# Issuing the loads of batch 3 at other places in GpSimd's order

## The chip, the core and the metric

The kernel runs on one core of a Trainium2 chip. Five engines work side by side, each through its own queue in order: TensorE (PE, with its weight loads shown as PEld), VectorE (DVE), ScalarE (ACT), GpSimd (POOL) and SyncE (SP). The metric is device time in microseconds (us); the median over runs is what is compared. One execution is profiled.

## The reference, cut to what matters

```
phi(x) = [exp(x @ w_phi - max|x @ w_phi|), exp(-x @ w_phi - max|...|)]
kv  = phi(k)^T v          z = sum over s of phi(k)         (per batch and head)
att = phi(q) kv / (phi(q) . z + 1e-6)
x   = att, heads side by side: 4608 tokens x 512
h   = x @ w_in            (512 -> 2048)
g   = h if h > 0, else exp(min(h, 0)) - 1
out = g @ w_out           (2048 -> 512)
```

There are 8 batches, 8 heads, 576 tokens in each batch and 64 numbers per head. Inputs and output are float32 in memory; the matmuls are bf16.

## The kernel before, in words

The attention is cut into 16 groups of four heads, two groups to a batch, so batch 3 is groups 6 and 7. For each batch, k, q and v are loaded from memory by one transfer each (`load`, line 213, issued at line 216), with a cast to bf16 on the way, and the issuing engine is GpSimd. The tiles `kn`, `qn` and `vn` come from a pool of two buffers each: the tile of batch 3 takes the buffer of batch 1. For groups from 4 on, k and q are transposed by transfers which SyncE issues (`t_dma`, lines 252 to 269), and the transposed `kT` and `qT` feed the matmuls of `k_mm` (line 294), `m_mm` (lines 353 and 368) and `q_mm` (lines 476 and 488). GpSimd also scales v (`v_scale`, line 331), copies the sums' weights (`v_ones`, line 340), and splits the q maxima of groups 0 to 3 into a high and a low half (`m_split`, lines 421 and 422). `kv_mm` (line 516) and `x_mm` (lines 549 and 565) then give the attention output; SyncE transposes that into `xT` (`x_dma`, lines 656 and 663).

The second part runs in 9 chunks of 512 tokens, mixed with the attention of later groups. For each of 16 column tiles, `h_mm` (line 672) fills a PSUM bank, `h_exp` (683, ScalarE) takes its exponential, `h_min` (688, GpSimd) clamps it at 1, and `h_elu` (692, VectorE) joins it with the bank and so lets go of the bank. `o_mm` (700) multiplies with `w_out`, `o_copy` (710) and `o_store` (716) bring the result out. Chunk 0 is worked in half tiles of 256 columns.

The order of everything is written out by hand in the string `ORDER`. Each letter takes the next item of one list of steps, so `e`, `f` and `g` issue the next load of k, q and v, and `E` the next v scaling, and a digit after a letter names the PSUM bank. The order of the letters is the order in which the program is emitted, and with it the order on each engine; nothing reorders it afterwards. Waits between engines are put in from what the instructions read and write.

```
e=(load, [("k", 0, 0, 1), ("k", 0, 1, 2), ("k", 0, 2, 4)]
   + [("k", *x) for x in all_batches[1:]]),
```

The transfers that GpSimd issues share eight completion semaphores in turn, and so do those that SyncE issues. A transfer waits at issue for the one eight places before it in its own series.

Of the kernel before, what the change touches and what calls it, by code (L numbers as in the profile page):

```python
# [19 lines left out]
DFFUV*M2NW6XBBP5Q*M0S4TTM2NNEU6j1kEEUV*j0k*OP2QS4TTM1NW6Xl0S2l1Y4ZTTj5km*mY7ZOP6Q*W3XS0TTp7A5Cp2  # L20
qrqrM3NS0TTissBp4qrj7kA0p3p2CsBqql6mrsrM4Nsp7p3BBM0Nqqp6p2DqqrrrA4BensssOCp0qY7Z*p3qp1qrsrrssrsE
W6XBl2m*p0p4qM2qrsrP1p5Q*DqES6TNM0NsS2TTTM0NFErsEFY6Zp7qrOsA0BBA2BU4UVp7qp6CP5Q*qBt4S0Tforrssp7q
p5CTrsqp6qW2XW0p7ttXDqS2TA0ngrsErsrsEp5p6p7qrtTCp2qFqrrBsp3qqrp5u*BsqssrsrsDFp4qp7qrsErsS0TTS2TT
t6ttA0zzU4CoEUVA2CBBtuBBW4W0p7t6vzXXzzzzM2NA4DqBenvzftrsM0NM2Np7qrstA0BBBCDM2Ntu*O*P7Q*Ct5S2TTt
M6S0TTEEFNtM6NEFU3S0ogEUVA6CtW3TTBBDEp1p0p2XW6Xuqrqqp5qp3p4p7p6srsA0nerrfqqrsssqrsBBM2NqO*rrp5p4
p2qrCsqssDrqp1qp7P3Q*qsp6p5rrssErsFqA2BBM0NCEqp4rrssqrsFt7S0TtS2M5TTTNvvzzzzS0oTTtA5CEU2US0tVu*B
BDFETTwW2XW4Xvt6A0BBCS2Ttttu*S0M4TTA2CDTFt7ttM0NBBA4BBM2NNCEEEgfDFEEztU0UV*A2CDzzp6qBup5qrrW0xR
t4tBp7qEEressoM0M2p6qrtNNW0xp5qsstu*S2M0p7p6TTrsRNqwp4qqrsS2TTyW0xrrssyp5p7qrqrS2TTnnA0CRp6qvvzo
# [793 lines left out]
```

## Time and profile before

| what | value |
|---|---|
| median of 13 runs | 365.07 us |
| lowest and highest | 362.66 and 369.19 us |
| the profiled execution, its own time | 362.66 us |
| its span, first to last instruction | 360.9 us |
| granted TensorE clock | 0.998 |
| PE busy | 340.7 us, 94% of the span |
| DVE, ACT, POOL busy | 268.9, 250.5 and 212.4 us |
| loads issued by GpSimd, bytes written | 18.35 MB |
| transfers issued by SyncE and ScalarE | 20.56 MB |

The profiled execution is the fastest of those shown; 1.8 us of its time lie outside the span. In the views, L216 is line 216 of the kernel; a row of the timeline has the start, the busy time, the engine, the line, the operation with its tiles, and how often it was repeated without a gap. In brackets stands the idle time ahead of it, with what ended it. SPq and POOLq are rows of issuing.

### The profile page before, as it was taken

How to read it: one execution, taken by the hardware profiler on the slowest of the kernel's cores; microseconds unless marked ns; L12 is line 12 of the kernel's file. 1: busy time of each engine (PE TensorE's matmuls, PEld its weight loads, DVE VectorE, ACT ScalarE, POOL GpSimd, SP SyncE). 2: the span in 40 equal slices, each digit the busy share in tenths (PEclk: the TensorE clock that was granted, in tenths of full speed). 3: DMA queues.
4: the chain of work that ended last, by engine and by line, in shares of the span. 5: the costliest groups of instructions: out<-in, count | busy, mean ns of one | idle time of the engine just before them, and what ended most of it. 6: DMA issues, size and time to landing. Idle time of an engine off the chain costs nothing.

```text
span 360.9 us, 9853 instructions
## 1 busy us (share of the span) xinstructions
PE 340.7 (94%) x3912; PEld 187.0 (52%) x3960; DVE 268.9 (75%) x470; ACT 250.5 (69%) x480; POOL 212.4 (59%) x328
## 2 busy tenths in 40 slices
PE   4788899999999999999999999999999999999994
PEld 3576676554455455545455445544555444444442
DVE  4989986978977998789988999988677914543430
ACT  3998978877898598877967987887855405533401
POOL 8754977358818669386868584767826505432400
PEclk9999999999999999999999999999999999999999
DMA  7999998999667964599578994441214221112123
GB/s 106 200 213 172 200 174 142 171 183 141 151 83 115 206 114 86 100 172 166 109 99 143 127 165 67 84 89 31 52 31 91 65 60 29 29 29 60 26 49 74
DMA packets 68479, 39.72 MB, mean 110 GB/s; under 512 B 48336, under 2 KB 62800, under 8 KB 68432
## 3 DMA queue, kind: packets, MB, share of 16 engines
q0 software_dynamic: 15856, 18.35, 32.7%
q1 hardware_dynamic: 52416, 20.56, 31.6%
q8 instruction: 31, 0.51, 0.6%
q10 hardware_dynamic: 160, 0.16, 0.1%
q14 instruction: 16, 0.13, 0.1%
HBM read 36.77 MB, written 9.44 MB: 128 GB/s over the span
## 4 chain that ended last, share of the span: by engine, by line
PE 80%; DVE 8%; ACT 6%; issue 3%; DMA 1%; POOL 1%; ACTq 0%; POOLq 0%; DVEq 0%
PE banks L700 34%; PE banks L672 28%; PE banks L516 5%; PE banks L549 3%; PE banks L476 2%; ACT EK L305 2%; PE banks L294 2%; DVE gT L692 2%; PE banks L353 2%; DVE mk L312 2%; DVE mq L395 2%; PE banks L565 2%; ACT Eq L500 1%; ACT e_sb L683 1%; DMA kn<-in_k_dram 1%
## 5 line engine op out<-in xcount | busy, mean ns | idle before, releaser
L688 POOL TENSOR_SCALAR e_sb<-e_sb 128x512 f32<-128x512 f32 (+1 forms) x160 | 89.9, 572 | 88.1 <-ACT e_sb L683 83.9
L700 PE MATMUL banks<-w_out_sb,gT 128*128 128x512 bf16 x549 | 131.1, 379 | 3.5 <-issue 2.7
L692 DVE SCALAR_TENSOR_TENSOR gT<-e_sb,banks 128x512 bf16<-128x512 f32 (+1 forms) x160 | 94.8, 625 | 36.0 <-POOL e_sb L688 35.5
L672 PE MATMUL banks<-xT,w_in_sb 128*128 128x512 bf16 (+1 forms) x557 | 119.7, 355 | 1.9 <-DVE mq L395 0.9
L683 ACT ACTIVATE e_sb<-banks 128x512 f32<-128x512 f32 (+1 forms) x160 | 87.0, 565 | 36.7 <-PE banks L672 31.9
L672 PEld LDWEIGHTS <-w_in_sb 128*128 128x128 bf16 x640 | 58.9, 98 | 57.8 <-issue 1.9
L700 PEld LDWEIGHTS <-gT 128*128 128x128 bf16 x576 | 52.8, 98 | 61.1 <-issue 2.4
L305 ACT ACTIVATE EK<-banks 128x768 bf16<-128x768 f32 x96 | 73.5, 814 | 13.4 <-PE banks L294 8.8
L500 ACT ACTIVATE Eq<-banks 128x768 bf16<-128x768 f32 (+2 forms) x96 | 72.8, 819 | 12.8 <-PE banks L476 7.8
L331 POOL TENSOR_TENSOR vs<-vn,em 128x576 bf16<-128x576 bf16 x64 | 73.1, 1154 | 12.6 <-ACT em L322 12.0
L312 DVE TENSOR_REDUCE mk<-banks 128x6 f32<-128x768 f32 x48 | 45.1, 951 | 5.4 <-PE banks L294 2.9
L710 ACT COPY o_sb<-banks 128x512 f32<-128x512 f32 x21 | 12.4, 590 | 34.5 <-PE banks L700 32.1
L381 DVE TENSOR_REDUCE mx<-banks 128x6 f32<-128x768 f32 (+1 forms) x30 | 30.6, 1036 | 3.4 <-PE banks L353 3.2
L615 POOL TENSOR_TENSOR xj<-xs,recj 128x448 bf16<-128x448 f32 (+1 forms) x23 | 20.5, 893 | 13.2 <-DVE recj L610 12.3
L594 DVE TENSOR_TENSOR xs<-banks,e 128x455 f32<-128x455 f32 (+1 forms) x30 | 18.1, 603 | 9.3 <-PE banks L549 8.2
L516 PE MATMUL banks<-vs,EK 64*128 64x65 bf16 x1152 | 21.5, 191 | 0.1
L516 PEld LDWEIGHTS <-EK 64*128 64x128 bf16 x1152 | 20.0, 94 | 2.3 <-DVE mx L381 0.8
L549 PEld LDWEIGHTS <-Eq 128*128 128x128 bf16 x400 | 15.9, 98 | 6.2 <-issue 0.3
L599 DVE TENSOR_TENSOR xs<-banks,xs 128x455 f32<-128x455 f32 (+1 forms) x30 | 18.3, 610 | 1.1
L294 PE MATMUL banks<-w_sb,kT 64*128 64x128 bf16 x288 | 16.6, 227 | 2.4 <-DVE kT L247 1.8
L710 DVE COPY o_sb<-banks 128x512 f32<-128x512 f32 x15 | 10.3, 684 | 11.1 <-PE banks L700 11.1
L549 PE MATMUL banks<-kv_sb,Eq 128*128 128x65 bf16 x400 | 17.1, 194 | 0.1
(67 smaller groups left out, 248.4 us busy)
## 6 DMA issues: line engine op xcount, KB each, us to landing
out_dram<-o_sb SPq DMA_DIRECT2D x71, 128.0 KB, 2.4
kn<-in_k_dram POOLq DMA_DIRECT2D x7, 576.0 KB, 9.1
qn<-in_q_dram POOLq DMA_DIRECT2D x7, 576.0 KB, 7.9
vn<-in_v_dram POOLq DMA_DIRECT2D x7, 576.0 KB, 8.3
w_in_sb<-in_moe_w_in_dram POOLq DMA_DIRECT2D x2, 1024.0 KB, 20.0
w_out_sb<-in_moe_w_out_dram POOLq DMA_DIRECT2D x1, 2048.0 KB, 16.3
qn<-in_q_dram POOLq DMA_DIRECT2D x2, 288.0 KB, 7.4
vn<-in_v_dram POOLq DMA_DIRECT2D x2, 288.0 KB, 8.1
```

Of the source, the lines that this page charges most:

```text
L305: nc.scalar.activation(EK[:, sg, 6 * c:6 * c + 6, :].rearrange("p (i r) f -> p r i f", r=2), st["pk", n, c], ACT.Exp, scale=1.0 - 2.0 * sg,)
L312: nc.vector.tensor_reduce(mk[:, 6 * c:6 * c + 6].rearrange("p (i r) -> p r i", r=2), st["pk", n, c], axis=AX.X, op=ALU.max, apply_absolute ...
L331: nc.gpsimd.tensor_tensor(get(("vs", n), new_vs)[:, sg, r, 0:D], st["v", n // 2][:, 2 * (n % 2) + pr], st["em", n][:, sg, r].unsqueeze(2). ...
L381: nc.vector.tensor_reduce(mq.rearrange("p (v r) -> p r v", r=2)[:, :, v0:v1], st["pm", n, c][:, :, 0:v1 - v0, :], axis=AX.X, op=ALU.max, a ...
L500: nc.scalar.activation(Eq[:, sg, :, :, p0 * D:p1 * D].rearrange("p h r x -> p r h x"), st["pq", n, c][:, :, 0:(p1 - p0) * P].rearrange("p ...
L516: nc.tensor.matmul(kv[:, hi, pr, sg, :], EK[rows, sg, pr * NS + s, :], vs[rows, sg, pr * NS + s, :], start=(s == 0), stop=(s == NS - 1),)
L549: nc.tensor.matmul(pn[:, sg, v - v0, :], Eq[:, sg, hi, par, i0 * D:(i0 + 2) * D], kv_sb[:, hi, pr, sg, :], start=True, stop=True,)
L672: nc.tensor.matmul(ph, w_in_sb[:, ct, jt * P:(jt + 1) * P], xT_of(ch)[:, ct, h0:h1], start=(ct == 0), stop=(ct == N_CT - 1),)
L683: nc.scalar.activation(e_sb, st["ph", ch, jt, h0], ACT.Exp)
L688: nc.gpsimd.tensor_scalar(e_sb, e_sb, 1.0, 0.0, op0=ALU.min, op1=ALU.max)
L692: nc.vector.scalar_tensor_tensor(gT[:, jt, h0:h1], st["e", ch, jt, h0], -1.0, st["ph", ch, jt, h0], op0=ALU.add, op1=ALU.max,)
L700: nc.tensor.matmul(po, st["gT", ch][:, jt, tt * P:(tt + 1) * P], w_out_sb[:, jt, :], start=(jt == 0), stop=(jt == N_JT - 1),)
```

## The change

Three letters move in `ORDER`; the rest of the kernel is the same. The load of k of batch 3 moves to just after the second v scaling of group 3. The load of q moves to a place behind two clamps of chunk 0 that follow it. The load of v moves ahead to a place behind the clamp of column tile 14, where the other two had been a few steps earlier. The splits of q maxima of groups 2 and 3 are issued by GpSimd in both kernels. The order of instructions on PE, DVE, ACT and SP is the same in both.

```diff
-p5CTrsqp6qW2XW0p7ttXDqS2TA0ngrsErsrsEp5p6p7qrtTCp2qFqrrBsp3qqrp5u*BsqssrsrsDFp4qp7qrsErsS0TTS2TT
-t6ttA0zzU4CoEUVA2CBBtuBBW4W0p7t6vzXXzzzzM2NA4DqBenvzftrsM0NM2Np7qrstA0BBBCDM2Ntu*O*P7Q*Ct5S2TTt
-M6S0TTEEFNtM6NEFU3S0ogEUVA6CtW3TTBBDEp1p0p2XW6Xuqrqqp5qp3p4p7p6srsA0nerrfqqrsssqrsBBM2NqO*rrp5p4
+p5CTrsqp6qW2XW0p7ttXDqS2TA0ngrsErsrsEep5p6p7qrtTCp2qFqrrfBsp3qqrp5u*BsqssrsrsDFp4qp7qrsErsS0TTS2
+TTt6ttA0zzU4CoEUVA2CBBtuBBW4W0p7t6vzXXzzzzM2NA4DqBnvztrgsM0NM2Np7qrstA0BBBCDM2Ntu*O*P7Q*Ct5S2TTt
+M6S0TTEEFNtM6NEFU3S0oEUVA6CtW3TTBBDEp1p0p2XW6Xuqrqqp5qp3p4p7p6srsA0nerrfqqrsssqrsBBM2NqO*rrp5p4
```

On GpSimd's queue this reads as follows (lines without a sign are context):

```diff
 L331 TensorTensor vs<-vn,em 128x9x64
+L216 DMACopy kn<-in_k_dram 128x4x576
 L688 TensorScalarPtr e_sb<-e_sb 128x256
 L340 TensorCopy vs<-em 128x2x9
-L688 TensorScalarPtr e_sb<-e_sb 128x256 x5
+L688 TensorScalarPtr e_sb<-e_sb 128x256 x2
+L216 DMACopy qn<-in_q_dram 128x4x576
+L688 TensorScalarPtr e_sb<-e_sb 128x256 x3
...
 L331 TensorTensor vs<-vn,em 128x9x64
-L216 DMACopy kn<-in_k_dram 128x4x576
-L216 DMACopy qn<-in_q_dram 128x4x576
-L688 TensorScalarPtr e_sb<-e_sb 128x256 x2
+L688 TensorScalarPtr e_sb<-e_sb 128x256
+L216 DMACopy vn<-in_v_dram 128x4x576
+L688 TensorScalarPtr e_sb<-e_sb 128x256
...
 L340 TensorCopy vs<-em 128x2x9
-L216 DMACopy vn<-in_v_dram 128x4x576
 L331 TensorTensor vs<-vn,em 128x9x64 x2
```

## The prediction

> **What bounds the kernel now.** I read the page first: the shares of the engines, then the chain of work that ended last. After it came the table of stretches around the loads that move, and the timelines of POOL, PE, DVE and SP between 50 and 92 us.
>
> ```profile
> PE 340.7 (94%) x3912; PEld 187.0 (52%) x3960; DVE 268.9 (75%) x470; ACT 250.5 (69%) x480; POOL 212.4 (59%) x328
> PE 80%; DVE 8%; ACT 6%; issue 3%; DMA 1%; POOL 1%; ACTq 0%; POOLq 0%; DVEq 0%
> 50.00:60.00 10.00, 9.79 (x115) 6.89 (x114) 8.04 (x19) 7.60 (x22) 7.78 (x17) 1.00 1.16 182
> 60.00:70.00 10.00, 9.79 (x179) 6.12 (x178) 7.83 (x14) 7.23 (x14) 4.03 (x7) 1.00 0.83 135
> 70.00:80.00 10.00, 9.63 (x171) 5.74 (x173) 8.11 (x13) 7.71 (x14) 6.23 (x10) 1.00 1.17 181
> ```
>
> The first two lines say that TensorE is the bound, over the span and along the chain; DMA and POOL end 1% of the chain each. The other three are stretches, with the busy us of PE, PEld, DVE, ACT and POOL, then clock, DMA share and GB/s. PE lacks 0.21, 0.21 and 0.37 us of each 10. A gain in this region can only come out of those gaps. A loss can be as large as the delay of something that PE really waits for.
>
> Now GpSimd's own rows. The three moved loads stand at 61.91, 62.73 and 74.55:
>
> ```profile
> 52.99 1.14 POOL L331 TENSOR_TENSOR vs<-vn,em 128x576 bf16<-128x576 bf16 x1
> 54.94 0.40 POOL L688 TENSOR_SCALAR e_sb<-e_sb 128x256 f32<-128x256 f32 x1 [0.81 <-ACT e_sb L683]
> 55.91 0.77 POOL L688 TENSOR_SCALAR e_sb<-e_sb 128x256 f32<-128x256 f32 x2 [0.36 <-ACT e_sb L683]
> 57.17 0.77 POOL L688 TENSOR_SCALAR e_sb<-e_sb 128x256 f32<-128x256 f32 x2 [0.49 <-ACT e_sb L683]
> 58.46 0.40 POOL L688 TENSOR_SCALAR e_sb<-e_sb 128x256 f32<-128x256 f32 x1 [0.53 <-ACT e_sb L683]
> 61.91 0.83 POOL L216 DMA_DIRECT2D kn<-in_k_dram  x1
> 62.73 0.75 POOL L216 DMA_DIRECT2D qn<-in_q_dram  x1
> 67.09 0.40 POOL L688 TENSOR_SCALAR e_sb<-e_sb 128x256 f32<-128x256 f32 x1 [3.61 <-ACT e_sb L683]
> 69.85 0.40 POOL L688 TENSOR_SCALAR e_sb<-e_sb 128x256 f32<-128x256 f32 x1 [2.35 <-ACT e_sb L683]
> 74.55 0.84 POOL L216 DMA_DIRECT2D vn<-in_v_dram  x1
> 75.41 1.17 POOL L331 TENSOR_TENSOR vs<-vn,em 128x576 bf16<-128x576 bf16 x1
> 80.84 1.15 POOL L331 TENSOR_TENSOR vs<-vn,em 128x576 bf16<-128x576 bf16 x1 [4.27 <-ACT em L322]
> ```
>
> The reader is to see the brackets: POOL waits for ScalarE on both sides of every moved load, so each issue of 0.75 to 0.84 us sits beside idle time, before and after the move.
>
> **The change part by part.** It adds and removes no work. Three issues of 0.83, 0.75 and 0.84 us leave their places and come back elsewhere.
>
> *Leaving 61.91 and 62.73.* This frees 1.58 us, after which POOL idles 3.61 us for ScalarE: worth 0. *Leaving 74.55.* The scaling at 75.41 starts 0.84 us earlier. The matmuls of L516 that need it start at 76.70, directly behind the matmuls of L488 ahead of them in PE's queue, so they gain 0. POOL then idles for 4.27 us anyway: worth 0.
>
> *k, at about 54.13.* The issue follows the scaling that ends at 52.99 + 1.14 = 54.13 and ends at 54.13 + 0.83 = 54.96. The next clamp started at 54.94 after 0.81 us of idling. It comes 0.02 to 0.03 us later, and the 0.36 us of idling ahead of 55.91 swallow that: 0. Without that cover the price would be 0.83 us on the clamps.
>
> *q, at about 56.67.* The pair of clamps that starts at 55.91 ends at 56.68; the issue runs until about 57.44. The next pair started at 57.17 and now starts 0.27 us late, to end at 58.21. The clamp at 58.46 had 0.53 us of idling ahead of it, so the delay dies there on POOL. Behind the delayed pair stand DVE and then PE:
>
> ```profile
> 56.76 1.63 DVE L692 SCALAR_TENSOR_TENSOR gT<-e_sb,banks 128x256 bf16<-128x256 f32 x4
> 58.90 0.92 DVE L692 SCALAR_TENSOR_TENSOR gT<-e_sb,banks 128x256 bf16<-128x256 f32 x2 [0.51 <-POOL e_sb L688]
> 58.57 0.33 PE L476 MATMUL banks<-qT,w_sb 64*128 64x384 bf16 x2
> ```
>
> The run of four is column tiles 7 to 10. The fourth started at about 58.0 and ended at 58.39; now its clamp ends at 58.21, so it ends at about 58.66. It frees bank 3, into which the matmuls of L476 at 58.57 write (the step `S2`: banks 2 and 3). They move to about 58.70, or 0.13 us. From below 0, if the matmul has other slack; from above 0.27, the whole delay. I take 0.15. The pair at 58.90 hangs on the undelayed clamp and stays.
>
> *v, at about 67.5.* It follows the clamp that starts at 67.09 and ends at about 68.3; the next clamp started at 69.85 after 2.35 us of idling: 0. The issue waits for GpSimd's own scaling of group 3, which is done at 61.97.
>
> *Waits of the issues.* The buffers that k and q take are read last by TensorE's transposes (L240), the last at 31.2 us for k and 38.7 us for q. The order of the loads among themselves is kept, and with it the transfer eight places back that each waits for. Those date from before 50 us. So no new wait stands in POOL's queue.
>
> *The transfers.* Here lies what could cost more. Each load moves 512 packets of about 1.1 KB. While such loads are in flight, SyncE's transposes barely move:
>
> ```profile
> q0 software_dynamic: 1015, 1.15, 89.7%
> q1 hardware_dynamic: 667, 0.39, 23.0%
> q1 hardware_dynamic: 2993, 0.73, 70.4%
> q1 hardware_dynamic: 2533, 0.65, 126.4%
> ```
>
> These are packets, MB and share of the 16 engines: the first two for 64 to 73 us (k and q of batch 3 in flight), the third for 56 to 62 us, the fourth for 73 to 76 us, when the loads are through and the backlog runs off. A transpose issued at 63.87 took 10.5 us to land, against 3.2 us for the `qT` of group 5 issued at 61.23.
>
> After the change the loads run earlier. The load of v of batch 2 is through at about 56.2. At the 164 packets per us of 53 to 56 us, k takes until 59.3 and q until 62.4. In those 6.2 us the transposes get about 667 / 9 x 6.2 = 460 packets of the 2,993 that they had in 56 to 62. The other 2,530 then need the 3 us of the fourth line: 65.4. Then comes `qT` of group 5, about 1,150 packets, some 1.4 us at the pace of 62 to 64, and a last part of a microsecond to land: about 67.5 instead of 64.4. TensorE first reads it at 70.47 (L368), so 3 us are left.
>
> `kT` of group 5 would land at about 63 to 64 instead of 59.5, for a reader at 70.08. SyncE waits for the transfer eight places back: its issue at 67.16 for the `kT` of 54.29, the one at 71.58 for `qT` of group 5. Both would have landed. `xT` of chunk 1 (last piece issued at 70.11, landed 5.6 us later, read at 79.04) meets one load, v, in place of two. `qT` of group 6 (landed by 84.3, read at 86.84) now runs beside no load and comes earlier, without anybody waiting. Sum of the transfers: 0.
>
> *A rule against it.* The Trainium skill (SBUF — State Buffer, "SBUF: two separate sides") says that VectorE instructions in a two-port mode keep GpSimd from writing descriptors of its transfers, and gives about 620 ns growing to 3,100 ns. k and q move from a stretch where DVE waits into one where it is busy. By that rule q could cost an estimated 2.5 us more on POOL, 2.3 us of it on the bank. The trace has a load at 49.95 in a busy DVE stretch at 0.78 us, and all 28 loads lie between 0.54 and 0.84 us. DVE reads PSUM in nearly all rows here. I take the row: nothing.
>
> **Sum.** 0.15 us on the profiled execution of 362.66 us: 362.8. That execution is 2.4 us under the median of 365.07, which it shares its work with, so the forecast is 365.07 + 0.15 = 365.2.
>
> **The rivals.** *Slower: `qT` of group 5 comes late (30%).* If transposes starve as long as the worst row, 10.5 us, and SyncE is held up by another 1.9 us at the issue ahead (its `kT` issue at 54.29 took 3.17 us, the `qT` one 1.31), it lands at 61.23 + 1.9 + 10.5 = 73.6, 3.2 us too late. This decides from a landing after 70.47, over 9.2 us from today's issue; each us after it is a us on PE, since PE has hardly a gap. It would give 366.4 to 368.3. For it speaks that 2,993 packets wait ahead of it; against it, that DMA stands nearly still from 60 to 62 (share 0.05), which takes up half a load.
>
> *Faster (15%).* With v's transfer away from 76 to 81 us and the issue out of the way at 74.55, the waits up to 90 us shrink. The gaps of PE between 60 and 90 us add up to 0.21 + 0.37 + 0.32 = 0.9 us. All of it gives 364.3, which is still within 0.5%. More than 0.5% needs executions other than the profiled one to stall on these transfers; 13 runs from 362.66 to 369.19 leave that open.
>
> *The change does not do what it says.* If the loads are taken in their order behind the one of v of batch 2, k lands later than its new issue suggests. By the above it still lands near 60 instead of 71; nobody needs it before `kT` of group 6 at 71.58, so this ends at 365.1.
>
> **How the numbers follow.** No effect beyond tenths of a us, with the second and third rival's small gains: 55%. A difference of 0.5% (1.8 us) is about what a measurement of this kernel can tell from none. Slower by more 30%, from the late transpose. Faster by more 15%. The range reaches from 362.8, the profiled sum and the lower runs, to 368.3, the late transpose at its worst.
>
> **What would show it.** Right: the load of k at about 54.1 and q at about 56.7 in POOL's rows; the clamps of 57.17 at about 57.45; the L476 matmuls of 58.57 later by 0.1 to 0.2 us; `qT` of group 5 landing before 70; PE busy at 9.6 us or more in each 10 from 50 to 90. Wrong: an idle gap of PE ahead of L368 or L294 near 70 us ended by DMA, L216 rows well over 0.84 us, or a chain in which DMA holds several per cent.

## The result, and the profile after

The changed kernel takes 370.54 us (median of 11 runs, 368.74 to 382.88), the kernel before 366.13 us (median of 48, 362.53 to 371.91). The ratio is 1.0165, with a 95% interval of 1.0127 to 1.0203: slower by 1.65%. The forecast was 365.2 us, no change, and its range ended at 368.3. Executions of one kernel can spread by 9 us and more; the ratios use those within 1.5% of a kernel's fastest, and the medians given here use all. The experiments trace much of that spread to the place where the loss arises.

The page of the kernel after, its busy times and the chain that ended last:

```profile
PE 344.1 (94%) x3912; PEld 189.5 (52%) x3960; DVE 269.6 (73%) x470; ACT 250.8 (68%) x480; POOL 212.5 (58%) x328
PE 79%; DVE 8%; ACT 4%; issue 3%; DMA 3%; POOL 2%; SPq 0%; DVEq 0%; POOLq 0%; ACTq 0%
```

The span went from 360.9 to 367.9 us. POOL's busy time is unchanged, PE's rose by 3.4 us though its instructions are the same, and DMA went from 1% to 3% of the chain. The stretches of the kernel after say where:

```profile
50.00:60.00 10.00, 9.90 (x122) 7.25 (x123) 7.85 (x19) 7.60 (x22) 9.03 (x18) 1.00 1.25 154
60.00:70.00 10.00, 9.01 (x161) 5.61 (x163) 4.91 (x11) 7.32 (x13) 3.92 (x6) 1.00 1.32 164
70.00:80.00 10.00, 6.08 (x48) 2.96 (x48) 7.12 (x10) 2.95 (x7) 3.85 (x7) 0.83 1.04 173
80.00:90.00 10.00, 9.79 (x180) 5.98 (x177) 5.50 (x10) 8.19 (x14) 3.88 (x6) 1.00 0.41 75
```

PE's column, the second number, falls to 6.08 us of 10 between 70 and 80 us, and the clock behind the busy times to 0.83. Everything before and after has its old pace: on ScalarE, instruction for instruction, the two profiles are 0.71 us apart up to 59 us, 0.89 at 65, 7.16 at 72, and about 7.05 from 79 to the end. One place lost the time. Two rows of the waits between 50 and 95 us (total, times, longest):

```profile
DVE xp L582 <- DMA xT_last<-xp: 4.9, 1, 4.9
PE banks L368 <- DVE xp L582: 3.6, 1, 3.6
```

VectorE's normalisation of group 3 (`x_div`, L582) waited 4.9 us for a transfer, and TensorE 3.6 us for VectorE. The same SyncE issues, the normalisation and three groups of matmuls in the kernel before:

```profile
54.29 3.17 SPq L266 DMA_TRANSPOSE kT<-kn  x1
57.51 1.26 SPq L656 DMA_TRANSPOSE xT<-xp  x1
58.82 2.31 SPq L663 DMA_TRANSPOSE xT_last<-xp  x1
66.62 0.82 DVE L582 TENSOR_TENSOR xp<-banks,rec 128x640 bf16<-128x640 f32 x1
67.24 1.04 PE L700 MATMUL banks<-w_out_sb,gT 128*128 128x512 bf16 x4
68.21 0.51 PE L368 MATMUL banks<-w_sb,qT 64*128 64x128 bf16 x12
70.97 0.81 PE L700 MATMUL banks<-w_out_sb,gT 128*128 128x512 bf16 x3 [0.16 <-issue]
```

The timelines of SyncE, of VectorE and of TensorE, kernel after:

```profile
56.67 3.61 SPq L266 DMA_TRANSPOSE kT<-kn  x1
60.34 5.22 SPq L656 DMA_TRANSPOSE xT<-xp  x1
65.61 1.23 SPq L663 DMA_TRANSPOSE xT_last<-xp  x1
66.94 2.74 SPq L266 DMA_TRANSPOSE qT<-qn  x1
```

```profile
67.28 0.22 DVE L580 RECIPROCAL rec<-den 128x10 f32<-128x10 f32 x1
72.36 0.82 DVE L582 TENSOR_TENSOR xp<-banks,rec 128x640 bf16<-128x640 f32 x1 [4.87 <-DMA xT_last<-xp]
73.10 0.95 DVE L395 TENSOR_REDUCE mq<-banks 128x6 f32<-128x768 f32 x1
```

```profile
68.64 1.04 PE L700 MATMUL banks<-w_out_sb,gT 128*128 128x512 bf16 x4
73.24 0.34 PE L368 MATMUL banks<-w_sb,qT 64*128 64x128 bf16 x6 [3.56 <-DVE xp L582]
74.10 0.37 PE L368 MATMUL banks<-w_sb,qT 64*128 64x128 bf16 x6 [0.52 <-DVE mq L395]
75.24 1.91 PE L700 MATMUL banks<-w_out_sb,gT 128*128 128x512 bf16 x4
78.03 0.81 PE L700 MATMUL banks<-w_out_sb,gT 128*128 128x512 bf16 x3 [0.16 <-issue]
```

The story in these rows: SyncE's issue of `kT` of group 5 lasts 3.61 us and that of the first `xT` of group 2 lasts 5.22, against 3.17 and 1.26 before. (The `kT` issue itself starts 1.67 us late, beyond the 0.71 us by which this execution runs late from its beginning.) So the small transpose `xT_last` of group 2 is issued at 65.61 instead of 58.82, and it lands 6.6 us later, at 72.2 instead of 62.2. The tile `xp` has three buffers, and the second half of group 3 writes into the one that this transpose reads. The normalisation waited for that, until 72.36. TensorE's next matmuls (L368, 73.24) start as it ends and lets go of its banks; the ones behind them waited another 0.52 us for VectorE's `m_max` (L395), which stands behind the normalisation in order.

Part of the loss comes after the wait. The same stretches in pieces of 2 us, kernel after:

```profile
72.00:74.00 2.00, 0.34 (x6) 0.20 (x6) 1.64 (x3) 0.00 (x0) 0.00 (x0) 1.00 1.25 231
74.00:76.00 2.00, 1.90 (x12) 1.04 (x12) 2.00 (x4) 0.46 (x2) 0.00 (x0) 0.57 1.16 262
76.00:78.00 2.00, 1.87 (x15) 0.82 (x15) 1.49 (x4) 0.95 (x2) 1.90 (x5) 0.58 0.74 149
78.00:80.00 2.00, 1.98 (x16) 0.89 (x15) 1.99 (x3) 1.53 (x5) 1.95 (x3) 1.00 0.71 140
```

The granted clock is 0.57 and 0.58 for about 4 us after the gap, and four matmuls of L700 take 1.91 us in place of 1.03.

The sum closes, from the starts of the same matmuls in both profiles. The L700 group at 67.24 before stands at 68.64: 1.40 us late, 0.71 of them there since 20 us into the program, 0.18 from the late clamps, 0.51 not explained (0.34 of it is a gap ahead of the matmuls of L565, which the trace puts down to issue). From it to L368 it takes 4.60 us instead of 0.97: 3.63 us, the wait. From L368 to the L700 group at 78.03 (70.97 before) it takes 4.79 instead of 2.76: 2.03 us, of which 0.52 is a wait for VectorE and the rest the clock. Together 7.06 us.

### The profile page after: what moved, and what is told of

Same layout as the page of the kernel before. It is cut to its first block, busy times and chain, and to the rows that moved or that the text cites. A ratio compares the mean times of both kernels' runs of the same rounds, so it can differ in the third digit from the quotient of the medians.

```text
span 367.9 us, 9854 instructions
## 1 busy us (share of the span) xinstructions
PE 344.1 (94%) x3912; PEld 189.5 (52%) x3960; DVE 269.6 (73%) x470; ACT 250.8 (68%) x480; POOL 212.5 (58%) x328
## 4 chain that ended last, share of the span: by engine, by line
PE 79%; DVE 8%; ACT 4%; issue 3%; DMA 3%; POOL 2%; SPq 0%; DVEq 0%; POOLq 0%; ACTq 0%
PE banks L700 33%; PE banks L672 27%; PE banks L516 5%; PE banks L549 3%; PE banks L476 3%; PE banks L294 2%; DVE gT L692 2%; DVE mk L312 2%; PE banks L353 2%; DMA xT_last<-xp 2%; ACT EK L305 1%; PE banks L240 1%; DVE mq L395 1%; PE banks L368 1%; POOL e_sb L688 1%
## 5 line engine op out<-in xcount | busy, mean ns | idle before, releaser
L700 PE MATMUL banks<-w_out_sb,gT 128*128 128x512 bf16 x549 | 132.0, 381 | 3.5 <-issue 2.7
L700 PEld LDWEIGHTS <-gT 128*128 128x128 bf16 x576 | 53.0, 98 | 61.6 <-issue 3.1
L615 POOL TENSOR_TENSOR xj<-xs,recj 128x448 bf16<-128x448 f32 (+1 forms) x23 | 20.5, 893 | 13.2 <-DVE recj L610 12.2
L516 PE MATMUL banks<-vs,EK 64*128 64x65 bf16 x1152 | 22.4, 194 | 0.0
L516 PEld LDWEIGHTS <-EK 64*128 64x128 bf16 x1152 | 20.9, 97 | 2.0 <-DVE mx L381 0.8
```

Source lines behind the costliest of these rows:

```text
L516: nc.tensor.matmul(kv[:, hi, pr, sg, :], EK[rows, sg, pr * NS + s, :], vs[rows, sg, pr * NS + s, :], start=(s == 0), stop=(s == NS - 1),)
L700: nc.tensor.matmul(po, st["gT", ch][:, jt, tt * P:(tt + 1) * P], w_out_sb[:, jt, :], start=(jt == 0), stop=(jt == N_JT - 1),)
```

## The experiments

Theory 1 (called 1a in the later expectations): k and q, issued early, fill the DMA engines while `kT` of group 5 and `xT` of group 2 are queued; SyncE's issues drag, and the first reader that notices stalls PE. Theory 2: the early load of v does it. Theory 3: the late clamps do it. In the diffs only the letters that move are shown; `n` is `t_dma` of k.

**k alone.**

```diff
-ngrsErsrsEp5p6p7q ... DqBenvz
+ngrsErsrsEep5p6p7q ... DqBnvz
```

> Only the load of k moves to its new place. Theory 1 (the two early loads together fill the DMA engines while kT of group 5 and xT of group 2 are queued; xT_last of group 2 then lands after the normalisation of group 3 wants its xp buffer): one load of 512 packets, about 3 us, delays the transposes by 3 to 4 us; xT_last of group 2 lands at about 66 instead of 62.2 and qT of group 5 at about 68 instead of 64.4, both just inside what the readers leave (66.6 and 70.5): 0 to +0.7 us. Theory 2 (the early load of v, in flight from 70 us on, keeps the late transposes from landing): 0. Theory 3 (the 0.27 us of clamp delay, amplified by the order): 0.

Measured: ratio 0.9988 (0.9941 to 1.0035); median 368.53 us against 367.49 for the kernel before in the same job, 363.56 to 379.6. In the profile `qT` of group 5 was issued at 62.12 and landed 7.5 us later, 2.2 us before its reader at 71.85, and L582 did not wait. That execution is as theory 1 has it. The median of all and the long executions are above what it allowed: 8 of 20 took longer than any of the 55 of the kernel before. That k takes the reserve away and these executions then miss it is the likely reason, but none of them was profiled.

**q alone.**

```diff
-TCp2qFqrrBsp3 ... nvzftrs
+TCp2qFqrrfBsp3 ... nvztrs
```

> Only the load of q moves to its new place; k and v stay. Theory 1: the same 3 us of load ahead of the transposes, a little later: 0 to +0.7 us. Theory 2: 0. Theory 3: the clamp pair is delayed by 0.27 us exactly as in the full change, so the full +6 us.

Measured: 0.9970 (0.9934 to 1.0006), median 364.08 us. The clamps are delayed as in the full change, and the loss is not there: theory 3 falls. The median is even 3.4 us under the 367.49 of the kernel before, and 3 of 20 executions are above 366 us against 33 of 55. Here, too, the two loads are apart, q early and k at 62.63.

**k and q, v at its old place.** The two edits above together.

> k and q at their new places, v back at its old one. Theory 1: the whole +6 us, with DVE's L582 waiting 4 to 5 us for xT_last<-xp. Theory 2: near 0. Theory 3: +6 us too (told apart by the load of q alone).

Measured: 1.0084 (1.0044 to 1.0125); median 370.28 us against 367.49. Two rows of its waits between 60 and 80 us:

```profile
DVE xp L582 <- DMA xT_last<-xp: 5.8, 1, 5.8
PE banks L368 <- DVE xp L582: 4.5, 1, 4.5
```

The two loads together bring the stall of theory 1; each alone does not in the profiled execution. But theory 1 wanted the whole loss, and by the ratios this is about half of it, 0.84% of 1.65%. The shortest execution here took 365.37 us, that of the full change 368.74. What the rest comes from is not shown; the early load of v is what remains different.

**v alone.**

```diff
-nvzftrs ... U3S0ogEUVA6C
+nvzftrgs ... U3S0oEUVA6C
```

> Only the load of v moves ahead, behind the clamp of column tile 14; k and q stay at 61.9 and 62.7. Theory 1: 0, since it comes after the transposes that matter. Theory 2: most of the +6 us, because v is then queued right behind k and q while the transposes wait.

Measured: four executions, 362.51, 371.83, 372.12 and 372.6 us: no ratio. The profiled one, of 371.83 us, had another stall: L582 did not wait, but `qT` of group 5 was issued at 63.27, behind k (62.78) and just ahead of q (63.61), and landed 14.5 us later; PE waited 6.5 us for it:

```profile
77.77 0.50 PE L368 MATMUL banks<-w_sb,qT 64*128 64x128 bf16 x6 [6.48 <-DMA qT<-qn]
```

It was measured again:

> v alone at its early place (about 67.5 us), measured in more rounds, since the first four executions lay between 362.5 and 372.6 us. Theory 1a: the early load of v does not touch kT, xT of group 2 and qT of group 5 as long as qT goes ahead of k and q; where qT falls behind k and q, v queued right after them makes it land later still (14.5 us in the profile of the first run, against 3.2). So the lowest executions are those of the kernel before, 362.5 to 363.5, and the longest are 1 to 2 us longer than there: median 366 to 370 us. Theory 2 (v is a cause of its own): no execution near the lowest of before, median over 370 us.

Measured: 0.9980 (0.9944 to 1.0016) from the short executions alone; the median of all is 369.77 us against 363.83. Seven of 22 executions lie at 363.06 to 363.96, the others at 368.6 to 374.4; the kernel before had 362.5 to 370.0 beside it. So v by itself does not force the loss, as theory 2 would have it, but it is not harmless: the long executions are up to 4 us longer, more than the 1 to 2 us expected. Whether they are also more frequent, 15 of 22 against 11 of 27 above 366 us, these runs do not settle.

**Four xp buffers**, in the changed kernel and in the one before.

```diff
-xpool = ctx.enter_context(tc.tile_pool(name="xpool", bufs=3))
+xpool = ctx.enter_context(tc.tile_pool(name="xpool", bufs=4))
```

> The changed kernel with four xp buffers instead of three, so that the normalisation of group 3 no longer writes into the buffer that xT_last of group 2 is still read from. Theory 1a (the transposes starve, and the xp buffer is only the first reader to notice; qT of group 5, which landed at 75.2 in the changed kernel, is the next): the wait of L582 for xT_last<-xp is gone, the matmuls of L368 for group 5 wait instead for qT<-qn from about 71.2 to 75.2, and 1.5 to 3 of the 6 us come back: 366 to 369 us. Theory 1b (the xp buffer is the whole cause): all 6 us come back, 363 to 365 us.

> The kernel before with four xp buffers: the control for the one above. Theory 1a: no difference, since the normalisation had 4.4 us in hand there; the longer executions of the kernel before, if they come from qT of group 5, stay. Theory 1b: the longer executions go, median near 363.5 us.

TensorE's rows of the changed kernel with four buffers, then of the kernel before with four:

```profile
71.91 0.34 PE L294 MATMUL banks<-w_sb,kT 64*128 64x128 bf16 x6
76.14 0.50 PE L368 MATMUL banks<-w_sb,qT 64*128 64x128 bf16 x6 [3.89 <-DMA qT<-qn]
76.57 1.89 PE L700 MATMUL banks<-w_out_sb,gT 128*128 128x512 bf16 x4
```

```profile
69.92 0.34 PE L294 MATMUL banks<-w_sb,kT 64*128 64x128 bf16 x6
73.76 0.34 PE L368 MATMUL banks<-w_sb,qT 64*128 64x128 bf16 x6 [3.50 <-DMA qT<-qn]
```

Measured for the changed kernel: median 369.31 us against 365.83, lowest 363.36, ratio 0.9992 (0.9947 to 1.0037) among its shorter executions. The wait of L582 is gone, and L368 waits 3.89 us for `qT` of group 5 instead, with the slow clock behind it (1.89 us). The buffer was only the first reader to notice (theory 1a); theory 1b, which wanted 363 to 365, falls. The buffer does count in part: 6 of 20 executions stay under 366 us, none of the 11 of the changed kernel did. The median came back less than expected: 3.5 us above the kernel before instead of 4.4.

For the kernel before: 366.41 against 365.83, ratio 1.0012 (0.9976 to 1.0048), no difference. Its profiled execution, of 367.79 us, is a long one and shows what makes them long: `qT` of group 5 comes late there too. SyncE's timeline of it:

```profile
56.93 4.68 SPq L266 DMA_TRANSPOSE kT<-kn  x1
64.58 2.55 SPq L266 DMA_TRANSPOSE qT<-qn  x1
```

In the profile of the prediction the `qT` issue was at 61.23, its packets went in 62 to 64 us, and the first packets of k went after 64. It won a race. Issued at 64.58, it falls behind k (61.75) and q (62.58). In this long execution the transfers were late before k and q came: between 52 and 54 us 53 packets moved, against 847 in the profile of the prediction, and the load of v of batch 2 landed 11.7 us after its issue instead of 7.4. What held them up is open.

**k and q later.** If that is so, moving the loads the other way must help.

```diff
-DqBenvzftrs
+DqBvztrefns
```

> k and q of batch 3 issued 5.6 us later than before, behind the clamp of column tile 14 (about 67.5 us), v at its old place; kT of group 6 goes to SyncE's queue two places later for that. Theory 1a: kT, xT and qT of groups 2 and 5 have the DMA engines to themselves up to about 69 us; qT of group 5 is never behind k and q, so the executions gather near the lowest of before, 362.5 to 364.5 us, unless xT of group 3, now queued beside both loads, lands after 79 us and costs L672 up to 2 us. A rival (early loads as such are not the point; what counts is how many transfers are in flight in all): no change in the spread, median 366 to 368 us.

SyncE's row of `qT`, GpSimd's rows of the two loads, and two stretches of this kernel:

```profile
62.16 1.31 SPq L266 DMA_TRANSPOSE qT<-qn  x1
```

```profile
67.45 0.83 POOL L216 DMA_DIRECT2D kn<-in_k_dram  x1
68.28 0.75 POOL L216 DMA_DIRECT2D qn<-in_q_dram  x1
```

```profile
60.00:70.00 10.00, 10.00 (x182) 6.13 (x182) 7.93 (x14) 7.22 (x14) 4.09 (x7) 1.00 0.75 92
70.00:80.00 10.00, 9.95 (x173) 5.71 (x173) 8.12 (x13) 7.72 (x14) 6.14 (x10) 1.00 1.20 207
```

Measured: 0.9952 (0.9919 to 0.9985); median 363.33 us against 365.83, and 12 of 13 executions between 362.39 and 365.19. `qT` landed 3.2 us after its issue. PE's gaps between 60 and 80 us are down to 0.05 us. `xT` of group 3 did not become late for its reader. Repeated in more rounds:

> The same kernel as the one with k and q at 67.5 us, measured again in more rounds. Theory 1a: median 363 to 364 us again, 0.3 to 0.8% below the kernel before, with most executions within 1.5 us of the lowest. If the first result was the luck of one chip: 365 to 367 us, as before.

Measured: 0.9924 (0.9900 to 0.9949); median 363.54 against 367.95 us, 21 of 22 executions between 362.47 and 365.19. This version is faster than the kernel before in both measurements, by 0.5 and 0.8%; it was not run beside the changed one.

The DMA queues of 60 to 66 us, first in the kernel after (loads, then transposes), then in the one with late k and q:

```profile
q0 software_dynamic: 670, 0.75, 113.8%
q1 hardware_dynamic: 315, 0.07, 20.1%
```

```profile
q1 hardware_dynamic: 1942, 0.69, 75.2%
```

Same 6 us, 315 packets of SyncE's queue against 1,942 (125 of these belong to output stores, none of the 315).

**q at 61.9, k at 67.5.**

```diff
-DqBenvzftrs
+DqBfvztrens
```

> q at about 61.9 us, k only at about 67.5 us, v at its old place: the two loads apart. Theory 1a: one load at a time holds the transposes up by 3 to 4 us only, as with k or q moved alone, so 362.5 to 365 us with few longer executions. The rival of the number in flight: as before, 366 to 368 us.

Measured: 0.9960 (0.9931 to 0.9990); median 363.82 us, 363.34 to 368.19. The profiled execution, 365.33 us, still has L368 waiting 1.38 us for `qT`, and here the clock stays at 1.00 (TensorE's timeline):

```profile
72.72 0.34 PE L368 MATMUL banks<-w_sb,qT 64*128 64x128 bf16 x6 [1.38 <-DMA qT<-qn]
72.99 1.04 PE L700 MATMUL banks<-w_out_sb,gT 128*128 128x512 bf16 x4
```

**Half of k and q early.** The loads of batch 3 are cut in two; the halves of group 6 go early, those of group 7 at 67.5 us.

```diff
+    HALVED = [
+        (b, *x) for b in range(1, B)
+        for x in ([(0, 2), (2, 4)] if b == 3 else [(0, H // 2)])
+    ]
...
-           + [("k", *x) for x in all_batches[1:]]),
+           + [("k", *x) for x in HALVED]),
...
-nvztrsM0
+nvztrefsM0
```

> k and q at the changed kernel's early places, but only the half of each that group 6 needs (288 KB); the other halves follow at 67.5 us, v at its old place. Two more issues on GpSimd. Theory 1a (bytes ahead of the transposes decide): as much is in the way as with one whole load, so 363.5 to 366 us, like k or q moved alone. The rival (the number of early transfers, or the early issues themselves, decide): as with k and q whole, 368 to 371 us.

Measured: 0.9970 (0.9938 to 1.0002); median 365.19 us against 367.95. Two early issues with half the amount do not bring the loss: what decides is the amount ahead of the transposes, not the number of issues. Bytes and packets were halved together, so these runs do not tell them apart.

## Why the prediction was wrong

The parts on GpSimd came true. Its rows of the kernel after:

```profile
54.80 0.83 POOL L216 DMA_DIRECT2D kn<-in_k_dram  x1
57.37 0.78 POOL L216 DMA_DIRECT2D qn<-in_q_dram  x1
58.18 0.78 POOL L688 TENSOR_SCALAR e_sb<-e_sb 128x256 f32<-128x256 f32 x2
59.17 0.40 POOL L688 TENSOR_SCALAR e_sb<-e_sb 128x256 f32<-128x256 f32 x1 [0.21 <-ACT e_sb L683]
68.45 0.83 POOL L216 DMA_DIRECT2D vn<-in_v_dram  x1
```

Counted from the 0.71 us by which this execution was late already, the clamp pair comes 0.30 us late (0.27 forecast), and the L700 group behind the L476 matmuls 0.18 us late (59.22 to 60.11; 0.15 forecast). The issues took 0.78 and 0.83 us, so the row was right and the rule on descriptors bore on nothing here.

*"Sum of the transfers: 0" failed, in three terms.* First, SyncE's issue time. The estimate let the transposes be queued at once and only land late. The runs showed SyncE standing in the issue itself while loads are in flight: 5.22 us for one `xT`, 6.37 for `kT` with k and q moved. `qT` of group 5 was forecast to be issued near 61.2 and to land at about 67.5; it was issued at 66.94 and landed at 75.2.

Second, a reader was left out. The text followed `kT`, `qT` and `xT` to TensorE, and did not ask whose buffer the transposes read. `xp` is released by the landing of `xT_last`, and the normalisation of group 3 needed it at about 66.6 in the profile before, 4.4 us after the landing at 62.2. That was the smallest reserve of all, and it broke first.

Third, how long loads and transposes hold each other up. The sum had v of batch 2 through at 56.2 us, k at 59.3 and q at 62.4; they landed at 59.7, 66.3 and 69.6, k and q 11.5 and 12.2 us after their issues. So the starved stretch was some 7 us longer than forecast. The transposes' share in it was put too high as well: 460 packets in 6.2 us, where 315 moved in 6 us. The 667 packets from which the 460 came hold 128 of output stores; without these it would have been about 370.

*The rival "`qT` of group 5 comes late" was the right mechanism with the wrong weight and price.* It was given 30% and at most 3.2 us, and in the changed kernel another reader stalled ahead of it. Its size lacked the clock: in the profile the waits of 3.56 and 0.52 us are followed by about 1.5 us of slow matmuls. The Trainium skill (TensorE: Matmul & The Clock Gate, "What's actually happening") has the clock at half after at least one idle window of about 3.4 us. The rows agree: gaps of 3.56, 3.50 and 3.89 us are followed by a slow clock, one of 1.38 us is not. The rival's 3.2 us lies just under that window, so the rule alone would not have raised it; the gap of 3.56 us, only slightly longer, had 1.5 us of slow matmuls behind it.

*The median was read as noise.* "13 runs from 362.66 to 369.19 leave that open" stood in the text, and the cause of the spread was not looked for. The race of `qT` against k and q explains it as far as the runs go: moving the two loads away took most of it, and the profiled execution was one that had won it. A reserve read from the fastest execution is likely to be among the largest that the kernel has.

*Faster did not come*: with v gone from 76 to 81 us nothing was gained there. Behind the stall the two profiles keep their distance of about 7.05 us.

## What to carry to other kernels

When a load moves, list everything that its bytes can delay on the DMA engines, SyncE's issues included, and for each delayed transfer both who reads its result and who waits to overwrite its source. Compare the reserves with the profile of a median execution. A wide spread of times in a kernel on one core can be a race that some executions lose, and moving the load away from it can be worth more than the change at hand. Price an idle gap of TensorE with the slow clock that may follow: here gaps of 3.5 us and more had one behind them.

## What the runs showed of the hardware

- SyncE's transpose issue, 1.2 to 1.4 us when DMA has room, grew to 6.37 us with k and q moved and to 6.77 us in the changed kernel with four buffers, while loads of GpSimd were in flight. In the profile before, the `xT` transposes behind k and q were issued in 1.2 to 1.9 us each and only landed late, so queueing alone does not explain it; what sets the limit is open.
- Beside a load the transposes often moved packet for packet with it: 212 packets beside 213 of the loads, 292 beside 287 and 232 beside 232, in the three stretches of 2 us from 60 to 66 us with k and q moved. A load's packet there held some 1.1 KB and a transpose's 0.25 KB. Without loads SyncE's queue moved 1,398 packets in 2 us (58 to 60, kernel before).
- Waits of TensorE of 3.50 and 3.56 us left the granted clock at 0.50 to 0.68 for about 4 us; one of 1.38 us left it at 1.00.
- One late transfer moved everything after it by a constant: in the profile after, the distance to the kernel before was 7.16 us at 72 us of the latter and about 7.05 us from 79 us to the end.
